# Local q and k of a sparse attention loaded in slices of every eighth token, and batch 0 masked through TensorE

## The chip, the core and the metric

The kernel runs on one core of a Trainium2 chip. The core has five engines that run side by side and wait for each other through semaphores: TensorE (PE; its weight loads are listed apart as PEld), VectorE (DVE), ScalarE (ACT), GpSimd (POOL) and SyncE (SP). DMA transfers are issued from the queues of SP, ACT and POOL and carried by 16 DMA engines. SBUF is the working memory of 128 partitions, PSUM the memory that TensorE writes its results to. The metric is the device time of one execution in microseconds; lower is better. The kernel before takes 322.0 us in the median of 8 runs (321.19 to 323.04).

## The reference

Two stages, one after the other. First a causal attention over 8 batches, 8 heads, 576 tokens and head dimension 64, in which heads 0 to 3 see only the last 32 tokens ("local") and heads 4 to 7 see every 32nd token ("strided"):

```
scores = scale * q @ k^T
rel = pos[:, None] - pos[None, :]
mask_local = (rel >= 0) & (rel < 32)
mask_strided = (rel >= 0) & (pos[None, :] % 32 == pos[:, None] % 32)
attn = softmax(where(mask, scores, -1e9));  y = attn @ v
```

Then the heads of a token are put side by side (4608 tokens by 512), and an MLP follows: h = x @ w_in (512 by 2048), g = h * tanh(softplus(h)) (the function Mish), out = g @ w_out (2048 by 512). Inputs and output are float32; the kernel computes in bfloat16.

## The kernel before

**Tiling of the attention.** Strided heads: token 8p + j lies in partition p (72 partitions, PN) and slice j (8 slices, CS), so that two slices of 64 elements make 128 columns. Their scores are 16 units of 72 by 72. Local heads: six windows of 96 queries against 128 keys (WQ, NW), for two pairs of heads, 12 units. Scores are made by `qk`, with keys on the partitions: PE multiplies kT by qT into PSUM, and ACT applies exp on the way to SBUF (P_s, P_l). `mask` multiplies P by a 0/1 mask on DVE. `pv` (one slice or window) and `pv2` (two) multiply P by v, with a column of ones that gives the denominator; DVE takes the reciprocal and scales into x_s or x_l. `xt` transposes x on PE, and ACT copies it into xT, the MLP's input.

**How q and k come to be transposed.** PE needs q and k with the head dimension on the partitions. Batch 0 and 1 are transposed on PE (`t_step`, `t_step_loc0`) with a copy from PSUM that puts the tokens in order. From batch 2 on DMA transposes do it: `transpose_str` issues two for the strided heads, of 16 units of 80 rows, and `transpose_loc` four for the local heads (k and q for two head pairs), each of six tiles of 96 consecutive tokens, straight into kTl and qTl. For that `load_qk_loc` loads local q and k of batch 0 and 1 with six consecutive tokens in a partition (96 partitions, rows of 1,536 bytes), and of later batches with token 96i + p in partition p (rows of 256 bytes). `cast_qk_loc` turns float32 into bfloat16 in the order that the transpose wants. The strided q and k come in through POOL's queue and are cast by the DMA (`load_qk_str`).

**Stages.** The order of every queue is written out by hand. A head part does the attention of batch 0. Then nine blocks t = 0 to 8 of 512 tokens follow. In block t PE first runs `mlp1(t)` (x @ w_in, eight groups, Mish on ACT), then `mlp2(t)` (g @ w_out, 16 groups), and between mlp2's groups the steps of the attention of batch t + 1 are put in (`attn_steps`). In block 0 PE also transposes batch 1, from the seventh entry of mlp1's list on. After mlp1's first group in block t >= 1, q and k of batch t + 1 are cast and `transpose_loc(t + 1)` is issued; after its third group v is cast and loaded, and `load_qk_str` is issued on POOL's queue (in block 1 for batches 3 and 4). In each such attention the first steps are the strided scores, their exp and their masks.

**POOL and SP in the early part.** Each queue runs in its own order. On POOL: memsets of P_l, loads of local q and k of batch 0 (lq0), memsets of rows 64 to 79 of ks and qs, a one-row copy `held` that waits for v of batch 0, the loads of w_in, casts of v, loads of batch 1's strided q and k, half of w_out, casts of batch 1's local q and k, and after a second `held` the other half of w_out. On SP: strided q and k of batch 0 in four loads (st0, which DVE casts into ks and qs), v, local q and k of batch 1, later all local and v loads, the DMA transposes and the output stores.

Of the kernel before, what the change touches and what calls it, by code (L numbers as in the profile page):

```python
# [18 lines left out]
CL, PL = 6, 96  # L19
# [5 lines left out]
def _consts():  # L25
# [5 lines left out]
    c = np.zeros((128, 128 + WQ + PN), np.float32)  # L31
    c[:, 0:128] = np.eye(128)
    c[:, 128:128 + WQ] = (rel >= 0) & (rel < STRIDE)
    c[:PN, 128 + WQ:] = (p[:, None] % 4 == p[None, :] % 4) & (p[:, None] <= p[None, :])
# [4 lines left out]
def kernel(ctx, tc, q, k, v, moe_w_in, moe_w_out, out):  # L39
# [15 lines left out]
    consts = const.tile([128, 128 + WQ + PN], BF16, name="consts_sb")  # L55
    ident = consts[:, 0:128]
    loc = consts[:, 128:128 + WQ]
    stm = consts[0:PN, 128 + WQ:128 + WQ + PN]
    vl32 = const.tile([128, 4, NW, D], F32, name="vl32")
    vs32 = const.tile([128, 4, CS, D], F32, name="vs32")  # L60
    ql32 = const.tile([128, 4, CL, D], F32, name="ql32")
    kl32 = const.tile([128, 4, CL, D], F32, name="kl32")
    ql = [const.tile([128, CL, 4, D], BF16, name=f"ql{i}") for i in range(2)]
    kl = [const.tile([128, CL, 4, D], BF16, name=f"kl{i}") for i in range(2)]
# [36 lines left out]
    def load_qk_loc(b):  # L101
        for dst, src in ((kl32, k), (ql32, q)):
            if b < 2:
                nc.sync.dma_start(
                    dst[0:PL].rearrange("p h j d -> p h (j d)"),
                    src[b, 0:4].rearrange("h (p j) d -> p h (j d)", j=CL),
                )
            else:
                nc.sync.dma_start(
                    dst[0:PL].rearrange("p h i d -> p (h i) d"),  # L110
                    src[b, 0:4].rearrange("h (i p) d -> p (h i) d", p=PL),
                )
# [40 lines left out]
    def cast_qk_loc(b, e_k, e_q):  # L153
        for e, dst, src in ((e_k, kl, kl32), (e_q, ql, ql32)):
            if b < 2:
                cast(e, dst[b % 2][0:PL].rearrange("p j h d -> p h j d"), src[0:PL])
            else:
                to = by_tile(dst[b % 2])
                for hp in range(2):
                    cast(  # L160
                        e, to[:, hp].rearrange("p i e d -> p e i d"), src[0:PL, 2 * hp:2 * hp + 2]
                    )

    def by_tile(x):

        return x[0:PL].rearrange("p j h d -> p (j h d)").rearrange(
            "p (t i e d) -> p t i e d", t=2, i=NW, e=2
        )

    def transpose_str(b):  # L170
        for src, dst in ((ks, kTs), (qs, qTs)):
            nc.sync.dma_start_transpose(
# [311 lines left out]
    with tc.manual_schedule():  # L484
# [43 lines left out]
        for i in range(3):  # L528
            a.qk([("s", i)], i)
# [131 lines left out]
```

The softmax here doesn't subtract the row's maximum and nothing guards it: scores larger than these inputs give would overflow.

## Time and profile before

| what | value |
|---|---|
| median of 8 runs | 322.0 us |
| the profiled execution's own time | 323.04 us |
| its span | 321.3 us |
| PE busy | 298.9 us (93%) |
| DVE busy | 127.7 us (40%) |
| ACT busy | 172.6 us (54%) |
| POOL busy | 41.3 us (13%) |
| first matmul of mlp1 | 26.9 us |
| first matmul of block 1, block 2, block 3 | 63.84, 100.03, about 132.6 us |

The span reaches from the program's first instruction to its last; the execution's own time has 1.7 us more around it. A profile's line gives the line of the code, the engine, the operation and the tiles as "out<-in". A wait is written "engine line <- what ended it: us in total, times, longest us". The chain of waits is followed back from the last instruction, at each step to what released it. In a table by stretches, each row has the stretch, its length, the busy time of each engine shown with its number of instructions, the clock that TensorE was granted (1.00 is full), the mean busy share of the DMA engines and the GB/s that they moved. In a timeline, each row has the start, the length, the engine (a name that ends in q is its queue), the operation, and in brackets the idle time before it and what ended it.

### The profile page before, as it was taken

What the parts mean: (1) busy time and instruction counts of PE and PEld (TensorE: products, weight loads), DVE (VectorE), ACT (ScalarE), POOL (GpSimd) and SP (SyncE); (2) the same over time, 40 slices, a digit from 0 to 9 for tenths busy, and PEclk for the clock granted to TensorE, in tenths of its full rate; (3) what the DMA queues carried; (4) which work ended last, traced back from release to release, by engine and by line L of the source; (5) the groups of instructions that cost most, each with busy time, mean ns of one, the idle gap of its engine ahead of it and who ended that gap; (6) DMA issues with size and microseconds to landing.
All of it is one profiled execution on the core that took longest, in us unless ns stands there. A gap on an engine that the chain in (4) does not pass through costs nothing.

```text
span 321.3 us, 5827 instructions
## 1 busy us (share of the span) xinstructions
PE 298.9 (93%) x2448; PEld 159.8 (50%) x2488; DVE 127.7 (40%) x332; ACT 172.6 (54%) x195; POOL 41.3 (13%) x50
## 2 busy tenths in 40 slices
PE   0678998999799999999999999999999999999996
PEld 0564455544345445544578655445544554444444
DVE  6672168600567038802880288028811830000000
ACT  2574563476437574656466646664667456315601
POOL 9288030145000000200020000000000000000000
PEclk9999999999889999999999999999999999999999
DMA  6999999999999999899989995896550101011012
GB/s 170 216 231 205 222 213 191 172 243 196 177 184 223 155 157 202 206 123 188 228 120 206 185 201 100 167 183 152 92 111 0 67 13 55 0 65 65 2 54 76
DMA packets 103114, 46.72 MB, mean 145 GB/s; under 512 B 85168, under 2 KB 95728, under 8 KB 103088
## 3 DMA queue, kind: packets, MB, share of 16 engines
q1 hardware_dynamic: 91648, 37.22, 64.6%
q0 software_dynamic: 11152, 8.92, 18.5%
q8 instruction: 19, 0.31, 0.4%
q10 hardware_dynamic: 288, 0.21, 0.2%
q14 instruction: 7, 0.06, 0.1%
HBM read 38.34 MB, written 9.44 MB: 149 GB/s over the span
## 4 chain that ended last, share of the span: by engine, by line
PE 81%; DVE 11%; DMA 4%; issue 2%; ACT 1%; SPq 0%; ACTq 0%
PE psh L428 38%; PE pso L467 27%; PE po L305 4%; PE pso L449 4%; DMA qTl<-ql 3%; PE ps L278 3%; DVE x_l L317 3%; DVE x_s L317 2%; PE trx L344 2%; DVE Pl L289 1%; DVE rden L316 1%; DVE ks L151 1%; DMA st<-in_k_dram 1%; PE trx L354 1%; PE tr L207 1%
## 5 line engine op out<-in xcount | busy, mean ns | idle before, releaser
L428 PE MATMUL psh<-xT,w_in 128*128 128x512 bf16 (+1 forms) x628 | 126.3, 359 | 0.8 <-issue 0.2
L467 PE MATMUL pso<-w_out,gT 128*128 128x512 bf16 x485 | 123.1, 382 | 1.7 <-issue 0.6
L433 ACT ACTIVATE gT<-psh 128x1024 bf16<-128x1024 f32 x72 | 73.6, 1023 | 44.0 <-PE psh L428 42.7
L428 PEld LDWEIGHTS <-w_in 128*128 128x128 bf16 x640 | 62.7, 98 | 62.2 <-issue 1.3
L467 PEld LDWEIGHTS <-gT 128*128 128x128 bf16 x512 | 43.9, 98 | 39.6 <-issue 1.1
L289 DVE TENSOR_TENSOR Ps<-Ps,consts_sb 72x864 bf16<-72x864 bf16 (+1 forms) x24 | 13.2, 551 | 89.7 <-ACT Ps L283 89.7
L149 ACT COPY xT<-trx 128x576 bf16<-128x576 bf16 x32 | 20.1, 639 | 37.7 <-PE trx L354 28.2
L474 ACT COPY osb<-pso 128x1024 f32<-128x1024 f32 x16 | 16.2, 1012 | 24.3 <-PE pso L467 13.8
L283 ACT ACTIVATE Ps<-ps 72x864 bf16<-72x864 f32 (+1 forms) x24 | 18.5, 803 | 15.3 <-PE ps L278 15.3
L316 DVE RECIPROCAL rden<-po 72x4 f32<-72x4 f32 (+1 forms) x100 | 17.4, 174 | 20.8 <-PE po L305 20.7
L317 DVE TENSOR_TENSOR x_s<-po,rden 72x256 bf16<-72x256 f32 x56 | 23.6, 421 | 1.9
L151 DVE COPY osb<-pso 128x512 f32<-128x512 f32 (+1 forms) x2 | 1.1, 558 | 54.5 <-PE pso L449 54.5
L283 ACT ACTIVATE Pl<-ps 128x960 bf16<-128x960 f32 (+1 forms) x24 | 18.7, 806 | 3.6 <-PE ps L278 3.5
L305 PEld LDWEIGHTS <-Ps 72*128 72x128 bf16 x256 | 14.2, 103 | 12.6 <-DVE Ps L289 2.6
L317 DVE TENSOR_TENSOR x_l<-po,rden 96x256 bf16<-96x256 f32 x44 | 18.5, 421 | 1.5
L305 PE MATMUL po<-vs,Ps 72*128 72x65 bf16 x256 | 17.9, 203 | 0.7 <-DVE x_s L331 0.5
L97 POOL DMA_DIRECT2D ks<-in_k_dram x7 | 6.2, 884 | 83.3 <-DMA kTs<-ks 83.3
L305 PE MATMUL po<-vl,Pl 128*128 128x65 bf16 x192 | 12.9, 201 | 2.2 <-DVE x_s L317 0.7
L449 PE MATMUL pso<-w_out,gT 128*128 128x512 bf16 (+1 forms) x79 | 14.0, 336 | 0.1
L305 PEld LDWEIGHTS <-Pl 128*128 128x128 bf16 x192 | 9.9, 103 | 6.5 <-DVE x_l L317 1.8
L289 DVE TENSOR_TENSOR Pl<-Pl,consts_sb 128x960 bf16<-128x960 bf16 (+1 forms) x24 | 13.1, 545 | 0.0
L449 PEld LDWEIGHTS <-gT 128*128 128x128 bf16 x80 | 7.8, 98 | 6.2
(70 smaller groups left out, 180.5 us busy)
## 6 DMA issues: line engine op xcount, KB each, us to landing
out_dram<-osb SPq DMA_DIRECT2D x16, 512.0 KB, 3.3
vl<-in_v_dram SPq DMA_DIRECT2D x7, 768.0 KB
vs<-in_v_dram SPq DMA_DIRECT2D x8, 576.0 KB
kl<-in_k_dram SPq DMA_DIRECT2D x7, 576.0 KB, 8.8
ql<-in_q_dram SPq DMA_DIRECT2D x7, 576.0 KB, 10.6
w_out<-in_moe_w_out_dram POOLq DMA_DIRECT2D x4, 512.0 KB, 15.4
ks<-in_k_dram POOLq DMA_DIRECT2D x7, 288.0 KB, 8.4
qs<-in_q_dram POOLq DMA_DIRECT2D x7, 288.0 KB, 9.8
```

What stands on the lines that cost most here:

```text
L149: nc.scalar.copy(out_, in_)
L278: nc.tensor.matmul(ps[:, e, o:o + w], lhsT=lhsT, rhs=rhs, start=True, stop=True)
L283: nc.scalar.activation(pt[0:n, :, 0:nw], ps[0:n, :, o0:o0 + nw], AF.Exp, scale=scale)
L289: meng.tensor_tensor(out=pm, in0=pm, in1=mk[0:n, :].unsqueeze(1).unsqueeze(1).to_broadcast([n, 2, nu, w]), op=ALU.mult,)
L305: nc.tensor.matmul(po[:, h, :], lhsT=pt[0:n, c0:c0 + 128], rhs=rhs, start=True, stop=True,)
L316: nc.vector.reciprocal(rden[0:m, :], po[0:m, :, D])
L317: nc.vector.tensor_tensor(out=dst.rearrange("p (h d) -> p h d", h=4), in0=po[0:m, :, 0:D], in1=rden[0:m, :].unsqueeze(2).to_broadcast([m, ...
L428: nc.tensor.matmul(ps[:, u, o:o + n], lhsT=w_in[:, cc, fc * 128:(fc + 1) * 128], rhs=xT[:, cc, a:a + n], start=(cc == 2), stop=(cc == 1),)
L433: nc.scalar.activation(gT[:, 2 * g:2 * g + 2, :], ps[:], AF.Mish)
L449: nc.tensor.matmul(p, lhsT=gT[:, fc, 128 * ot:128 * ot + 128], rhs=w_out[:, fc, c0:c1], start=(fc == 0), stop=(fc == 15),)
L467: nc.tensor.matmul(p[:, ot % 2, :], lhsT=gT[:, fc, 128 * ot:128 * ot + 128], rhs=w_out[:, fc, :], start=(fc == 0), stop=(fc == 15),)
L474: nc.scalar.copy(osb[:], p[:])
```

## The change

Local q and k take the layout of the strided ones in every batch: token 8p + j in partition p, slice j, 72 partitions with rows of 2,048 bytes. A DMA transpose then gives 16 units of 80 columns (two head pairs times eight slices) instead of tokens in order. There are two transposes a batch, into new tiles kTu and qTu, and a new step `in_order` copies them, reading every 80th column, into kTl and qTl. In block 1 this copy is on POOL, in later blocks on DVE, between mlp1 and mlp2. kl and ql have one buffer each instead of two. Batches 0 and 1, still transposed on PE, use eight slices of 72 instead of six of 96.

In the head part, the masks of batch 0 are no longer multiplied on DVE: a matmul of the identity by a bias matrix (0 or -30000, new columns of the constants) first fills the accumulator, and the scores are added to it without a new start. The copies of batch 0's local transposes go to DVE for head pair 0 and to ACT for pair 1. v's strided cast moves from DVE to POOL, the local v cast from ACT to POOL, the memsets of ks[1] and qs[1] from the start to block 0, and the order of pv, qk and xt steps is new.

```diff
     def load_qk_loc(b):
         for dst, src in ((kl32, k), (ql32, q)):
-            if b < 2:
-                nc.sync.dma_start(... 96 partitions, j=CL ...)
-            else:
-                nc.sync.dma_start(... "h (i p) d -> p (h i) d", p=PL ...)
+            nc.sync.dma_start(
+                dst[:].rearrange("p h j d -> p h (j d)"),
+                src[b, 0:4].rearrange("h (p j) d -> p h (j d)", j=CS),
+            )
...
+    def transpose_units(src, dst):
+        nc.sync.dma_start_transpose(dst[:, 0:16 * SU].rearrange("c (u n) -> c u n", u=16), src)
     def transpose_loc(b):
-        for hp in range(2):
-            for src, dst in ((kl, kTl[:, hp, 32:32 + S]), (ql, qTl[:, hp, :])):
-                nc.sync.dma_start_transpose(...)
+        for src, dst in ((kl, kTu), (ql, qTu)):
+            transpose_units(src[:].rearrange("p h j e d -> p (h j e d)"), dst)
+    def in_order(eng):
+        for src, dst in ((kTu, kTl[:, :, 32:32 + S]), (qTu, qTl[:])):
+            cast(
+                eng, dst.rearrange("c h (p j) -> c h p j", j=CS),
+                src[:].rearrange("c (h j n) -> c h n j", h=2, j=CS)[:, :, 0:PN, :],
+            )
...
+        def bias(self, kind, i, i_acc):
+            n, w, mk = (128, WQ, locb) if kind == "l" else (PN, PN, stmb)
+            nu = len(PARTS[kind][i])
+            ps = acc(i_acc, "ps")
+            for e in range(2):
+                nc.tensor.matmul(
+                    ps[:, e, 0:nu * w].rearrange("p (u c) -> p u c", u=nu), lhsT=ident[0:n, :],
+                    rhs=mk.unsqueeze(1).to_broadcast([n, nu, w]), start=True, stop=True,
+                )
+            return ps
-        def qk(self, parts, i_acc):
+        def qk(self, parts, i_acc, ps=None):
...
-                        nc.tensor.matmul(ps[:, e, o:o + w], lhsT=lhsT, rhs=rhs, start=True, stop=True)
+                        nc.tensor.matmul(
+                            ps[:, e, o:o + w], lhsT=lhsT, rhs=rhs, start=first, stop=True,
+                            skip_group_check=not first,
+                        )
...
+        sb = [a.bias("s", i, i) for i in range(3)]
         for hp in range(2):
             h = 2 * hp
             cast(Dv, qs[0][0:PN, h:h + 2, :], st0[1][:, h:h + 2, :])
             t_step(0, "s", "q", hp, Dv if hp else Sc)
         for i in range(3):
-            a.qk([("s", i)], i)
-        a.mask("s", 0, Dv)
-        cast(Dv, vs[0][0:PN, :, :, 0:D], vs32[0:PN])
-        a.mask("s", 1, Dv)
-        for x in (ks, qs):
-            Po.memset(x[1][64:SU], 0.0)
+            a.qk([("s", i)], i, sb[i])
+        cast(Po, vs[0][0:PN, :, :, 0:D], vs32[0:PN])
         Po.tensor_copy(held[:], vs[0][0:1, 3, 0, 0:4])
...
         cast_v_loc(0, Po, 0, 3)
+        cast_v_loc(0, Po, 3, 6)
...
         for hp in range(2):
-            t_step_loc0(kl0, kTl[:, hp, 32:32 + S], hp, Sc)
-        a.pv2("s", 0, 0)
-        a.mask("s", 2, Dv)
-        a.pv2("s", 2, 1)
+            t_step_loc0(kl0, kTl[:, hp, 32:32 + S], hp, Sc if hp else Dv)
+        lb = [a.bias("l", i, i) for i in range(2)]
         for hp in range(2):
-            t_step_loc0(ql0, qTl[:, hp, :], hp, Sc)
+            t_step_loc0(ql0, qTl[:, hp, :], hp, Sc if hp else Dv)
+        a.pv2("s", 0, 2)
+        a.qk([("l", 0)], 0, lb[0])
...
         def rest_of_w_out():
...
+            for x in (kl, ql):
+                Po.memset(x[64:SU], 0.0)
             cast_qk_loc(2, Po, Po)
...
+                at[1] += [lambda x=x: Po.memset(x[1][64:SU], 0.0) for x in (ks, qs)]
...
                     transpose_loc(t + 1)
+                    if t == 1:
+                        in_order(Po)
...
+            if t > 1 and t + 1 < B:
+                in_order(Dv)
             for i, g in enumerate(mlp2(t, gT, out_accs, fc_major=(t == 0), spare=spare)):
```

## The prediction

> **What bounds the kernel now.** I read the page first, then the waits of TensorE (PE), the chain of waits, the table by stretches, and the timelines of SP and POOL around the one long wait.
>
> ```profile
> span 321.3 us, 5827 instructions
> ...
> PE 298.9 (93%) x2448; PEld 159.8 (50%) x2488; DVE 127.7 (40%) x332; ACT 172.6 (54%) x195; POOL 41.3 (13%) x50
> ...
> DMA  6999999999999999899989995896550101011012
> ...
> PE 81%; DVE 11%; DMA 4%; issue 2%; ACT 1%; SPq 0%; ACTq 0%
> ```
>
> PE carries the end: 81% of the chain. DMA is full until about 240 us, yet holds only 4% of it. So time can be won or lost only where PE stands still, and the waits of PE show two such places: the start (8.5 us before the first transposes) and this one:
>
> ```profile
> PE ps L278 <- DMA qTl<-ql: 1.9, 1, 1.9
> ```
>
> ```profile
> 63.84:100.03 36.19, 33.94 (x265) 16.68 (x268) 12.28 (x38) 19.81 (x23) 8.03 (x10) 0.95 1.23 205
> 100.03:132.60 32.57, 32.08 (x265) 16.12 (x269) 15.86 (x43) 19.74 (x22) 1.41 (x2) 1.00 1.19 183
> ```
>
> Columns: stretch, length, busy PE, PEld, DVE, ACT, POOL, granted clock, DMA share, GB/s. Blocks 1 and 2 hold the same 265 matmuls, but block 1 takes 3.62 us more and has a mean clock of 0.95. The stretches inside it (length, PE, clock, DMA share, GB/s) tell why:
>
> ```profile
> 84.00:86.00 2.00, 0.74 (x17) 1.00 1.30 185
> 86.00:88.00 2.00, 2.00 (x10) 0.64 1.35 179
> 88.00:90.00 2.00, 2.00 (x10) 0.51 1.36 175
> ```
>
> PE waits from 83.3 to 85.2 us, then runs at half clock until 90.3. The wait costs 1.9, the clock about 1.7. And why is the transpose late?
>
> ```profile
> 73.91 0.72 POOL L97 DMA_DIRECT2D ks<-in_k_dram  x1
> 74.62 0.71 POOL L97 DMA_DIRECT2D qs<-in_q_dram  x1
> 75.32 0.70 POOL L97 DMA_DIRECT2D ks<-in_k_dram  x1
> 76.02 0.70 POOL L97 DMA_DIRECT2D qs<-in_q_dram  x1
> ```
>
> The fourth local transpose was issued at 74.80 and landed at 85.2; the third (73.49) landed at 78.3. Between them POOL's queue launched the strided loads of batches 3 and 4, which held about 91% of the DMA engines from 76 to 84 us.
>
> The start:
>
> ```profile
> 4.46 1.80 POOL L534 MEMSET ks<- 16x2048 bf16 x1
> 4.82 4.28 DVE L151 CAST ks<-st 72x1024 bf16<-72x1024 f32 x2 [1.13 <-DMA st<-in_k_dram]
> 6.20 2.35 POOL L534 MEMSET qs<- 16x2048 bf16 x1
> 9.02 1.27 DVE L151 CAST qs<-st 72x1024 bf16<-72x1024 f32 x2
> ```
>
> Two equal casts take 2.18 us each beside POOL's memsets and 0.68 without.
>
> **What the Trainium skill says.** "TensorE: Matmul & The Clock Gate", Part 1: after an idle window of some 3.4 us the clock halves, and as long a busy one restores it. The trace agrees on the halved clock and its length (86.7 to 90.3), though the wait was only 1.9 us. "SBUF — State Buffer", "SBUF: two separate sides": DVE in a two-port mode and GpSimd lock one port pair for a whole instruction; the 2.18 against 0.68 us agrees. "DMA: Bandwidth & Descriptors", "Why a DMA increments its semaphore by 16 and not by 1": a load runs on the largest number of engines up to 16 that divides the slowest dimension, so 72 partitions use 12 and 96 use 16. The completion records agree: each st load has 12 late increments (4.2 to 4.8 us for the first). "VectorE: DVE Perf Modes", "Mode 1× (REGULAR)": one element a cycle at 0.96 GHz whatever the stride. The strided copies kTl<-tr give 758 ns for 576 elements.
>
> **The change part by part.**
>
> *Strided loads of block 1.* in_order on POOL stands ahead of these four loads in POOL's queue, and waits for both new transposes. They can no longer collide. The transposes are issued after the two output stores (66.67 and 69.44 now, the second gated by the copy ending at 65.05). Bytes: 2 x 1,280 packets of 256 B for 4 x 576, +11%; the isolated pair of strided transposes at 222.09 landed both by 228.6 (6.5 us), the isolated local four at 231.91 by 238.6 (6.7), so the DMA time is equal. Three of four landed by 78.3 now; with the queue ahead of them shorter (below) I put both at 75 to 78. The copies have no row: 1,152 strided elements on POOL, nearest the 826 ns for 768 of vl, so 1.2 us each; GpSimd's worse case, twice that, 2.5. Done at 77.5 to 80.5, at worst 83; PE asks at 83.1. The wait goes, and with it the slow clock: **-3.6** (from 0, if the copies are late, to -3.6).
>
> *Local loads of batches 2 to 7.* 4,608 packets of 256 B (median 29 to 31 ns; kl and ql alone took 206.0 to 213.9 = 7.9 us) become 576 of 2,048 B on 12 engines: 48 an engine x 84 to 121 ns = 4.0 to 5.8 us. DMA gets 2 to 4 us a batch, SP's issues of 8 to 10 us shrink. PE waits for no load there, so 0 by itself; it pays for the rest.
>
> *in_order on DVE, blocks 2 to 6.* Two copies of 1,152 elements: 1.2 us at one a cycle plus about 0.1, 2.6 a block; casts of 72x1024 (676) for 96x768 (548) add 0.5. The cover:
>
> ```profile
> 117.30 0.60 DVE L289 TENSOR_TENSOR Ps<-Ps,consts_sb 72x864 bf16<-72x864 bf16 x1 [13.68 <-ACT Ps L283]
> ```
>
> DVE is idle 13.7 us before the first mask of each block. Behind the waiting copy stands only that mask, and behind it PE's first pv. The transposes landed at 115.9, 146.4, 176.3 and 206.0; masks at 117.3, 149.8, 182.4 and about 215. One copy (1.3) after the last landing just fits at 117.3, without the DMA relief. With two batches' relief (4 to 8 us by then), less up to 2 us of DMA idle while POOL holds back its loads, block 2 fits even 3.6 us earlier: **0** (bound: the second rival).
>
> *Start.* The four st loads landed at 4.8, 6.1, 7.5 and 8.9. Without memsets the k casts end at 6.8 instead of 9.1, the q casts at 9.6 instead of 10.3. But six bias matmuls (2,304 columns; PE is at half clock here, 427 ns for 512 columns at 27 us) add 1.9 us from 7.4 to 9.3, so qk starts near 11.1 as now. Then local k, landed at 13.5, holds PE in both kernels. From there: masks gone from DVE (0.60 + 0.60 + 0.44 + 0.64 + 0.64 + 0.34 = 3.3) and vs' cast moved to POOL (1.2), but PE gets another 1.9 us of bias. PE's work from 13.5, at half clock: transposes 2.4, bias 1.9, qk 1.5, pv 4.3, x transposes 2.5, plus waits: mlp1 starts at about 25.7 to 26.2, not 26.9. It is not kept: w_out's first part landed at 41.45 and PE asks at 42.86, slack 1.4. POOL now issues w_in after its own cast of vs (landed 13.3, cast 1.9), 0.5 us later, and engines 0 to 11 carry a third more bytes each of lq, kl and ql. I put that landing at 42.0 to 43.0, so **-0.3** (-1.2 to +1.0).
>
> *Block 0.* Memsets of kl and ql (1.8 each) follow POOL's loads at 44.5, beside DVE's cast of vs (44.92, 1.22). If locked out, the mask at 46.53 is up to 0.9 late and PE has 0.6 of slack: **+0.3** (0 to +0.9). The transposes, 8 x 72 for 6 x 96, take 0.42 either way (rows L207, L220). Casts on POOL end near 62, before they are asked for.
>
> *POOL's copies beside the first masks of block 1*: **+0.2** (0 to 0.9).
>
> Sum: -3.6 - 0.3 + 0.3 + 0.2 = **-3.4**. It is made against the profiled execution (span 321.3, 1.7 us around it: 323.04, the top of the runs shown). Carried to the median 322.0 it gives **318.6**.
>
> **Rivals.** (1) *The start pays.* If w_out isn't as late as I fear, or the denser PE gains full clock before mlp1 (its first four matmuls cost 0.43 instead of 0.21), another 1 to 2 us: 316.5 to 317.5. For: 3.3 us of masks are gone. Against: DMA is full from 6 us. (2) *Slower: DVE stands before a transpose.* With PE 3.6 us earlier, block 2's mask is due at 113.7, and qTu must land by 112.4. If the relief is under 2 us a batch, landing stays near 115: a wait of about 2.6 and the half clock after it, 1.7, in block 2, and since PE is early again, part of it in block 3 and 4: 3.6 gained, 5 to 6 lost, 323.5 to 324.5. It decides when the landing is later than the mask's due time less 1.3. For: DMA share is above 1.2 in those blocks. Against: 31 ns packets. (3) *Even*: the copies on POOL take above 2.5 us, or block 2 takes back what block 1 gave: 321 to 322.5.
>
> **Numbers.** A difference under 0.3% (1.0 us) can't be told from none. Forecast 0.53 (317.5 to 320), rival 1 0.14, even 0.15, slower 0.18. Faster 0.68 (the forecast, rival 1 and 0.01 of even), same 0.14, slower 0.18. The range leaves out most of rival 2 and the far end of rival 1: 316.6 to 322.8.
>
> **What would show it.** Right: no PE wait for a local transpose near 83 us, clock 1.00 in 84 to 90, block 1 at about 32.6 us; POOL's four loads after 77; two DVE copies of some 1.3 us each ending before the mask. Wrong: DVE's first mask waiting behind in_order with PE idle and a clock near 0.5 in block 2 or 3; POOL copies above 3 us; a wait of pso on w_out near 42 us; mlp1 starting after 27.

## The result, and the profile after

The changed kernel takes 327.8 us in the median of 11 runs (326.15 to 332.21), against 322.3 us before on the same chips: a ratio of 1.017 (95% interval 1.014 to 1.020). It is slower by 1.7%, on the other side of the forecast of 318.6 us, and outside its range. Ratios here leave out executions that lie over 1.5% above the fastest of the same kernel; medians don't.

The page of the changed kernel (span, busy shares, DMA in 40 slices, the chain):

```profile
span 326.1 us, 5884 instructions
...
PE 303.1 (93%) x2483; PEld 161.5 (50%) x2524; DVE 140.6 (43%) x340; ACT 170.5 (52%) x191; POOL 54.2 (17%) x58
...
DMA  6999999999999999999989975995480101011011
...
PE 72%; DMA 16%; DVE 7%; issue 1%; SPq 1%; POOL 1%; ACT 0%; POOLq 0%; ACTq 0%
```

PE does nearly the same work, but its part of the chain falls from 81% to 72%, and DMA's rises from 4% to 16%: PE now stands more, for data. Where, the table by blocks tells. Before, the row of block 0, which the prediction did not show:

```profile
26.90:63.84 36.94, 35.48 (x318) 18.86 (x323) 18.21 (x46) 17.96 (x21) 8.65 (x10) 1.00 1.24 201
```

After, blocks 0, 1 and 2:

```profile
27.77:72.07 44.30, 38.24 (x325) 19.82 (x331) 20.50 (x47) 17.66 (x21) 22.59 (x19) 0.96 1.16 202
72.07:104.56 32.49, 32.00 (x265) 16.08 (x269) 12.20 (x37) 19.80 (x23) 11.44 (x11) 1.00 1.10 205
104.56:137.04 32.48, 31.99 (x264) 16.07 (x268) 18.86 (x45) 19.75 (x22) 1.87 (x2) 1.00 1.05 174
```

Block 1 went from 36.19 to 32.49 us, as forecast: -3.7. But mlp1 starts 0.87 later, and block 0 takes 7.36 us more. Block 2 is the same: before, it ran from 100.03 to 132.51 us, so it took 32.48 and not 32.57. 0.87 + 7.36 - 3.70, plus 0.3 in all that follows, is the 4.8 us between the spans. The waits of PE, after:

```profile
PE po L315 <- DVE x_s L327: 4.1, 2, 3.0
PE tr L228 <- DMA lq<-in_k_dram: 2.7, 1, 2.7
PE ps L285 <- ACT Ps L293: 1.3, 1, 1.3
```

The first is the large one. DVE's timeline tells what held x_s up, before and after:

```profile
52.70 0.94 DVE L151 CAST vl<-vl 128x768 bf16<-128x768 f32 x1
```

```profile
59.86 0.96 DVE L151 CAST vl<-vl 128x768 bf16<-128x768 f32 x1 [3.48 <-DMA vl<-in_v_dram]
```

The local v of batch 1 landed at 59.8 us instead of 52.6. DVE's cast stood for it, the reciprocals behind that cast stood too, and PE behind them; the clock was then granted at 0.73 and 0.50 from 62 to 66 us:

```profile
62.00:64.00 2.00, 0.89 (x8) 0.50 (x7) 1.93 (x6) 0.00 (x0) 0.85 (x1) 0.73 1.73 191
64.00:66.00 2.00, 1.78 (x12) 0.97 (x12) 1.16 (x5) 0.00 (x0) 1.53 (x2) 0.50 0.93 184
```

These waits and that clock make some 4.6 us of block 0. The third wait, 1.3 us, is a table load. ACT's timeline before and after:

```profile
43.58 1.28 ACT L283 ACT_TABLE_LOAD   x1
```

```profile
47.92 1.28 ACT L293 ACT_TABLE_LOAD   x1 [2.10 <-PE ps L285]
```

Before, the table of Exp was loaded as soon as ACT had finished its last Mish: the load waits for a semaphore of DVE, long since given. After, it waits for PE's scores of batch 1, and PE waits for it. The other 1.4 us of block 0 is a longer half clock at the start of mlp1 (10 matmuls 427 ns apart instead of 4), which a second execution of the kernel before, below, has as well.

### The profile page after: what moved, and what is told of

It is laid out like the page before. It is cut to its first block, busy times and chain, and to the rows that moved or that the text cites. A ratio compares the mean times of both kernels' runs of the same rounds, so it can differ in the third digit from the quotient of the medians.

```text
span 326.1 us, 5884 instructions
## 1 busy us (share of the span) xinstructions
PE 303.1 (93%) x2483; PEld 161.5 (50%) x2524; DVE 140.6 (43%) x340; ACT 170.5 (52%) x191; POOL 54.2 (17%) x58
## 2 busy tenths in 40 slices
DMA packets 79826, 47.16 MB, mean 145 GB/s; under 512 B 58808, under 2 KB 68408, under 8 KB 79800
## 3 DMA queue, kind: packets, MB, share of 16 engines
q1 hardware_dynamic: 68360, 37.62, 57.3%
## 4 chain that ended last, share of the span: by engine, by line
PE 72%; DMA 16%; DVE 7%; issue 1%; SPq 1%; POOL 1%; ACT 0%; POOLq 0%; ACTq 0%
PE psh L438 34%; PE pso L477 26%; DMA vl<-in_v_dram 12%; PE pso L459 4%; DMA w_in<-in_moe_w_in_dram 4%; PE po L315 4%; PE ps L285 3%; DVE x_l L327 2%; DVE x_s L327 2%; DVE rden L326 1%; PE trx L354 1%; DVE Pl L299 1%; PE trx L364 1%; DVE vl L151 1%; POOL vl L151 0%
## 5 line engine op out<-in xcount | busy, mean ns | idle before, releaser
L438 PE MATMUL psh<-xT,w_in 128*128 128x512 bf16 (+1 forms) x628 | 127.7, 362 | 0.8 <-issue 0.2
L477 PEld LDWEIGHTS <-gT 128*128 128x128 bf16 x512 | 43.9, 98 | 39.6 <-issue 1.1
L149 ACT COPY xT<-trx 128x576 bf16<-128x576 bf16 x31 | 19.6, 638 | 41.5 <-PE trx L364 33.8
L299 DVE TENSOR_TENSOR Ps<-Ps,consts_sb 72x864 bf16<-72x864 bf16 (+1 forms) x21 | 11.6, 551 | 43.1 <-ACT Ps L293 43.1
L484 ACT COPY osb<-pso 128x1024 f32<-128x1024 f32 x16 | 16.2, 1012 | 22.7 <-PE pso L477 13.9
L327 DVE TENSOR_TENSOR x_s<-po,rden 72x256 bf16<-72x256 f32 x60 | 25.2, 421 | 2.1
L293 ACT ACTIVATE Ps<-ps 72x864 bf16<-72x864 f32 (+1 forms) x24 | 18.5, 803 | 12.7 <-PE ps L285 12.6
L151 DVE COPY osb<-pso 128x512 f32<-128x512 f32 (+1 forms) x2 | 1.1, 558 | 54.5 <-PE pso L459 54.5
L151 DVE COPY kTl<-kTu 128x1152 bf16<-128x1152 bf16 x5 | 6.4, 1277 | 29.1 <-DMA kTu<-kl 29.1
L327 DVE TENSOR_TENSOR x_l<-po,rden 96x256 bf16<-96x256 f32 x42 | 17.7, 421 | 1.4
L103 POOL DMA_DIRECT2D ks<-in_k_dram x7 | 5.5, 790 | 73.8 <-DMA kTs<-ks 73.8
L151 DVE CAST vl<-vl 128x768 bf16<-128x768 f32 x12 | 10.9, 942 | 3.5 <-DMA vl<-in_v_dram 3.5
```

Source lines behind the costliest of these rows:

```text
L149: nc.scalar.copy(out_, in_)
L151: eng.tensor_copy(out_, in_)
L293: nc.scalar.activation(pt[0:n, :, 0:nw], ps[0:n, :, o0:o0 + nw], AF.Exp, scale=scale)
L299: meng.tensor_tensor(out=pm, in0=pm, in1=mk[0:n, :].unsqueeze(1).unsqueeze(1).to_broadcast([n, 2, nu, w]), op=ALU.mult,)
L327: nc.vector.tensor_tensor(out=dst.rearrange("p (h d) -> p h d", h=4), in0=po[0:m, :, 0:D], in1=rden[0:m, :].unsqueeze(2).to_broadcast([m, ...
L438: nc.tensor.matmul(ps[:, u, o:o + n], lhsT=w_in[:, cc, fc * 128:(fc + 1) * 128], rhs=xT[:, cc, a:a + n], start=(cc == 2), stop=(cc == 1),)
```

## The experiments

Fifteen further kernels were run, and both kernels of the comparison a second time. Times are medians, ratios are against runs of the kernel before on the same chip, with 95% intervals; most kernels have four executions, the kernels with more are named. Figures of blocks and waits are those of one profiled execution of each. In all nineteen profiles blocks 3 to 7 take the same times within 0.05 us, e_late and e_fix apart: what differs lies in the start and in blocks 0 to 2.

### The change in halves

`e_b2only`: the kernel before with the new layout from batch 2 on alone.

```diff
 def load_qk_loc(b):
...
-            else:
-                nc.sync.dma_start(
-                    dst[0:PL].rearrange("p h i d -> p (h i) d"),
-                    src[b, 0:4].rearrange("h (i p) d -> p (h i) d", p=PL),
-                )
+            n, c = (PL, CL) if b < 2 else (PN, CS)
+            nc.sync.dma_start(
+                dst[0:n, 0:256 * c].rearrange("p (h x) -> p h x", h=4),
+                src[b, 0:4].rearrange("h (p j) d -> p h (j d)", j=c),
+            )
...
+                    if t == 1:
+                        in_order(Po)
...
+            if t > 1 and t + 1 < B:
+                in_order(Dv)
```

> The kernel before with the new local layout from batch 2 on alone (loads of 2,048-byte rows, two transposes, in_order); batches 0 and 1 and the start as before. The start theory (what is late comes from batches 0 and 1 or from the new order of the start): block 0 stays near 37 us, vl of batch 1 lands at 52 to 54 us, block 1 takes 32.6 us, time 318 to 319. The packet theory (kl and ql of batch 2, in rows of 2,048 bytes, crowd out the 256-byte packets of vl of batch 1): vl lands at 57 us or later, block 0 takes over 40 us, time 321 to 324.

Measured: 323.7 us in 20 executions, ratio 1.005 (1.002 to 1.008). vl of batch 1 landed at 48.7, so the packet theory falls; but block 0 took 39.08 us, not about 37, and the 318 to 319 us of the start theory aren't met either. Block 1 took 34.13 and block 2 33.01: half of the gain in block 1 is there against the first execution of the kernel before, none against the second (below), a wait of 1.6 us stays at its first masks, and the time is already slightly worse.

`e_layout` is the changed kernel with the old head part:

```diff
-        sb = [a.bias("s", i, i) for i in range(3)]
...
         for i in range(3):
-            a.qk([("s", i)], i, sb[i])
-        cast(Po, vs[0][0:PN, :, :, 0:D], vs32[0:PN])
+            a.qk([("s", i)], i)
+        a.mask("s", 0, Dv)
+        cast(Dv, vs[0][0:PN, :, :, 0:D], vs32[0:PN])
+        a.mask("s", 1, Dv)
...
```

`e_head` is the kernel before with the new head part, the same lines the other way round. `e_after_l96` is the changed kernel with the old layout in batches 0 and 1:

```diff
+            n, c = (PL, CL) if b < 2 else (PN, CS)
             nc.sync.dma_start(
-                dst[:].rearrange("p h j d -> p h (j d)"),
-                src[b, 0:4].rearrange("h (p j) d -> p h (j d)", j=CS),
+                dst[0:n, 0:256 * c].rearrange("p (h x) -> p h x", h=4),
+                src[b, 0:4].rearrange("h (p j) d -> p h (j d)", j=c),
             )
...
-            Po.dma_start(dst, src[0, 0:4].rearrange("h (p j) d -> p h (j d)", j=CS))
+            Po.dma_start(dst, src[0, 0:4].rearrange("h (p j) d -> p h (j d)", j=CL))
...
```

> The changed kernel with the old start: masks of batch 0 on DVE, v's strided cast on DVE, the second half of the local v cast on ACT, memsets at the start, steps in the old order. The layout is the new one in every batch. Theory of the 12 engines (72-partition loads of batches 0 and 1 fill twelve of sixteen engines ahead of w_in): the last part of w_in lands at 35 us or later, vl of batch 1 at 57 to 60, time 323 to 327. Theory of the start's order (POOL holds w_in back for v's cast): w_in lands near 34, vl near 53, time 318 to 319.5.

> The kernel before with the new start alone (bias matmuls, casts on POOL, copies on two engines, new order); the local layout stays the old one everywhere, so the wait of block 1 (1.9 us and the half clock after it) stays. Theory of the start's order: w_in lands at 36 or later, vl of batch 1 at 56 or later, block 0 over 40 us, time 325 to 330. Theory of the 12 engines: w_in lands at 34 to 35, vl at 52 to 55, time 321.5 to 324, what is over 322 from the table of Exp, which now is loaded behind the scores of batch 1 (up to 1.4 us).

> The changed kernel with batches 0 and 1 alone in the old local layout (96 partitions, six slices), all else as changed. Theory of the 12 engines: w_in lands at 34 to 35, vl of batch 1 at 52 to 55, time 318 to 321. Theory of the start's order: w_in at 36 to 37, vl at 57 to 60, time 325 to 328.

Measured: 327.3 (1.019, 1.010 to 1.028), 325.3 (1.010, 1.004 to 1.017) and 325.9 (1.011, 1.003 to 1.019). Neither theory fits: each half alone is slower, and where the early part was mended (block 0 at 38.73 and 39.37 us, vl at 48.7 and 46.8), the time was lost in block 2 instead. e_head has no loss in block 2; it keeps the collision (block 1 at 36.29) and has the wait for the table in block 0. The waits of PE in e_layout and in e_after_l96:

```profile
PE po L292 <- DVE Ps L276: 2.6, 1, 2.6
```

```profile
PE po L329 <- DVE Ps L313: 3.0, 2, 2.8
```

That is the rival that the prediction gave 0.18: DVE's first mask standing behind in_order, which waits for the transposes.

### What made block 1 slow

`e_hold` is the kernel before and, in block 1, one copy of four elements ahead of the strided loads:

```diff
                     if t + 2 < B:
                         load_v(t + 2)
+                    if t == 1:
+                        Po.tensor_copy(held[:], qTl[0:1, 1, 0:4])
                     for b in range(max(3, t + 2 + (t > 1)), min(t + 4, B)):
                         load_qk_str(b)
```

`e_loads_first` is the changed kernel with in_order of block 1 behind those loads:

```diff
                     transpose_loc(t + 1)
-                    if t == 1:
-                        in_order(Po)
...
                     for b in range(max(3, t + 2 + (t > 1)), min(t + 4, B)):
                         load_qk_str(b)
+                    if t == 1:
+                        in_order(Po)
```

> The kernel before with one line more: at block 1 POOL copies four elements of qTl, and so stands until the last local transpose has landed, before it launches the strided loads of batches 3 and 4. Old layout and old start throughout. Collision theory (these loads alone made the transpose late): the PE wait near 83 us and the half clock go, block 1 takes 32.5 to 32.8 us. If the early part is bound by the sum of DMA work, what is won comes back as a wait for a local transpose in block 2 and the time is 320.5 to 322; if not, it is 318 to 319. Layout theory (it is the two larger transposes that removed the wait): block 1 stays above 35 us.

> The changed kernel with POOL's in_order of block 1 behind the strided loads of batches 3 and 4 in its queue instead of ahead of them. Collision theory: qTu lands at 84 us or later, POOL's copies end after 88, PE waits 3 us or more near 90 us, time 329 to 333. Relief theory (fewer packets are what removed the wait, and holding the loads only wastes DMA time): qTu lands before 82, no wait, time 325 to 327.5.

Measured: e_hold 320.4 us in 20 executions, ratio 0.995 (0.992 to 0.997), the best kernel of this study; e_loads_first 327.1, ratio 1.012 (1.003 to 1.020). Block 1 of e_hold, and block 1 of e_loads_first:

```profile
65.45:97.94 32.49, 32.38 (x270) 16.08 (x268) 12.19 (x38) 19.80 (x23) 8.26 (x11) 1.00 1.22 205
```

```profile
67.75:104.05 36.30, 34.21 (x269) 16.70 (x268) 12.28 (x37) 19.80 (x23) 12.17 (x11) 0.95 1.07 196
```

With the old layout and the loads held back, block 1 takes 32.49; with the new layout and the loads ahead, 36.30, with a PE wait of 2.0 us and the half clock after it. The collision is shown from both sides, and the layout has no part in it. e_hold missed the 318 to 319 us expected where nothing comes back in block 2: block 2 has no wait, but its block 0 took 38.97 us. e_loads_first missed 329: PE's wait at the copies was 2.0 us and not 3 or more, and its block 2 has no wait, since PE was late already.

### A second execution of both kernels, and the table of Exp

> The kernel before itself, to see how much of its block 0 and block 1 is one execution's chance. The first profile had block 0 at 36.94 us and block 1 at 36.19. If half clock at the start of mlp1 falls by chance, block 0 is between 36.5 and 39.5 and block 1 takes back a part (33.5 to 36.3), with the sum between 71 and 74.

Measured: 322.4 us. Blocks 0 and 1:

```profile
26.90:65.28 38.38, 36.92 (x318) 19.22 (x323) 18.40 (x46) 17.96 (x21) 9.15 (x10) 1.00 1.25 196
65.28:99.41 34.13, 32.28 (x265) 16.14 (x268) 12.19 (x38) 19.80 (x23) 8.03 (x10) 1.00 1.22 199
```

Block 0 is 1.44 us longer and block 1 2.06 shorter than in the execution that the prediction read: the wait for qTl is 1.5 us, and no slow clock follows it. So the 3.6 us to be won in block 1 were the upper end; 1.6 (34.13 less 32.49) to 3.7 is what the two executions hold. The prediction read them in the slowest of its eight executions (323.04) and took them from the median. e_hold, whose median is 1.35 below that of the kernel before, fits the lower end.

> The changed kernel itself, unchanged, to see a second execution in full. If the late vl of batch 1 (59.8 us) is a property of the kernel, it lands at 57 to 61 us again and PE waits 4 us near 60. If it is one execution's chance, it lands at 47 to 53, and the time is lost in another place: a wait of 2.5 to 3 us in block 2 as the two relatives of it showed, with block 0 at 39 to 41 us.

Measured: 326.9 us, and another picture. vl landed at 51.9, block 0 took 40.17, block 1 32.49, block 2 34.08. DVE and PE at the first masks of block 2:

```profile
117.60 1.27 DVE L151 COPY kTl<-kTu 128x1152 bf16<-128x1152 bf16 x1 [11.24 <-DMA kTu<-kl]
119.00 1.27 DVE L151 COPY qTl<-qTu 128x1152 bf16<-128x1152 bf16 x1
120.20 1.11 DVE L299 TENSOR_TENSOR Ps<-Ps,consts_sb 72x864 bf16<-72x864 bf16 x2
```

```profile
PE po L315 <- DVE Ps L299: 1.5, 1, 1.5
```

So the changed kernel loses its time in one of two places: at vl in block 0, or, where PE comes through block 0 in time, at the transposes of batch 3 in block 2.

`e_preload` is the changed kernel with an explicit load of the table behind the last mlp1 group of block 0:

```diff
+            if t == 0:
+                Sc.preload_act_table(AF.Exp)
             for i, g in enumerate(mlp2(t, gT, out_accs, fc_major=(t == 0), spare=spare)):
```

> The changed kernel with an explicit load of the Exp table after the last mlp1 step of block 0, as it happened before the change on its own. If each stall of block 0 counts: the wait of 1.35 us behind the first scores of batch 1 goes and the time falls to 326.0 to 326.7. If vl of batch 1, which lands after it, decides: the wait for x_s grows by the same 1.3 us and the time stays at 327.5 to 328.

Measured: 328.0 us (1.017, 1.009 to 1.025): nothing won. The wait of 1.3 us for the table is gone from the list, and in its profile, the slowest of its four executions (330.6), this one has come up in block 2:

```profile
PE po L315 <- DVE Ps L299: 4.9, 2, 4.6
```

### Mending one part at a time

`e_late` is the changed kernel with in_order behind the first two masks:

```diff
                     at = attn_steps(t + 1, x, y)
+                    if t > 1:
+                        at[1].append(lambda: in_order(Dv))
...
-            if t > 1 and t + 1 < B:
-                in_order(Dv)
```

`e_split` is the changed kernel with every local load of q and k split (lq in the same way):

```diff
-            nc.sync.dma_start(
-                dst[:].rearrange("p h j d -> p h (j d)"),
-                src[b, 0:4].rearrange("h (p j) d -> p h (j d)", j=CS),
-            )
+            for p in (slice(0, 64), slice(64, PN)):
+                nc.sync.dma_start(
+                    dst[p].rearrange("p h j d -> p h (j d)"),
+                    src[b, 0:4].rearrange("h (p j) d -> p h (j d)", j=CS)[p],
+                )
```

`e_fix` is e_after_l96 with the edits of e_preload and e_late.

> The changed kernel with in_order of blocks 2 to 6 behind the first two masks of each block on DVE instead of ahead of them. Gate theory (the two copies tie the first masks to the landing of the transposes, and PE then stands in block 2): the wait of the first pv near 120 us goes or falls below 0.7 us, and the time falls by 1 to 3 us to 325 to 327; in an execution in which block 0 is late by itself nothing is won. If the transposes themselves are what PE lacks, the wait reappears one step on, at the scores of the local part, with the same length, and the time stays at 327 to 328.

> The changed kernel with each load of local q or k (72 partitions) issued as two, one of 64 partitions and one of 8, and nothing else. Theory of the 12 engines: the 64 partitions spread over sixteen engines, local k of batch 0 lands at 13.5 to 14.5 us instead of 15.4, the last part of w_in at 33.5 to 35 instead of 36.8 to 38.2 with its sixteen completions less than 2.5 us apart, mlp1 starts at 26.2 to 27.2, and the time falls by 1 to 3 us to 325 to 327. If the number of bytes is what counts, all of these stay within 0.5 us.

> The changed kernel with three parts mended at once: batches 0 and 1 in the old layout of 96 partitions, the Exp table loaded after the last mlp1 step of block 0, in_order of blocks 2 to 6 behind the first two masks. If these three are all that lost time, block 0 takes 37 to 39 us, block 1 and block 2 take 32.5 to 33, and the time is 318 to 321, below the kernel before. If the loss is the sum of DMA work ahead of block 2, a wait stays in block 1 or 2 and the time is 322 to 326.

Measured: 337.9 (1.051, 1.046 to 1.055), 332.9 (1.033, 1.027 to 1.038) and 336.3 us (1.045, 1.038 to 1.051). All three were expected to gain. e_late, PE's waits and DVE in block 2:

```profile
PE ps L285 <- DVE qTl L151: 8.1, 5, 1.6
```

```profile
121.96 0.60 DVE L299 TENSOR_TENSOR Ps<-Ps,consts_sb 72x864 bf16<-72x864 bf16 x1 [0.17 <-ACT Ps L293]
122.49 1.26 DVE L151 COPY kTl<-kTu 128x1152 bf16<-128x1152 bf16 x1
123.67 1.26 DVE L151 COPY qTl<-qTu 128x1152 bf16<-128x1152 bf16 x1
```

Behind the masks the two copies (2.5 us) stand in front of the local scores, in each of five blocks, for 1.6 us each. That prices the cover that the prediction named: ahead of the masks the copies are free when the transposes have landed, and right behind them they are not. e_fix pays the same, and 3.1 us in block 2. e_split: local k landed by 15.6, no earlier than in the changed kernel (15.4); PE waited 1.7 instead of 2.7 us for it because it came later itself. The last part of w_in came at 38.7 instead of 36.8, and PE waited 6.8 us in block 0. Splitting the loads, which also doubles their number in the queues, doesn't mend the start.

### Which transfer is late

`e_gate` is the changed kernel with kl and ql of batch 2 held on SP:

```diff
             Po.memset(x[0][64:SU], 0.0)
-        load_qk_loc(2)
...
             load_w_out(2, 4)
             load_qk_str(2)
+            nc.sync.dma_start(gate[:], w_out[0:1, 8, 0:256])
+            load_qk_loc(2)
```

`e_l96_gate` is e_after_l96 with this edit and that of e_preload; `e_head_hold` is e_head with the edits of e_hold and e_preload.

> The changed kernel with the loads of kl and ql of batch 2 held on SP until the third part of w_out has landed (a four-row copy that waits for it stands ahead of them), nothing else. Order theory (SP's loads of batch 2 run ahead of ks, qs of batch 2 and vl of batch 1): vl of batch 1 lands at 45 to 50 us, qs of batch 2 at 58 to 61 instead of 63 to 66, the DMA share of 60 to 72 us rises above 1.05, the transposes of batch 3 land by 117.5, and the time is 321 to 325. Start theory (half a megabyte less by 27 us is carried along): the transposes of batch 3 land at 118.5 or later and the time stays at 326 to 328.5.

> The changed kernel with batches 0 and 1 in the old layout of 96 partitions, the Exp table loaded after the last mlp1 step of block 0, and the same hold of kl and ql of batch 2; in_order stays ahead of the masks. Order theory: no PE wait above 0.7 us in blocks 0 to 2, block 3 starts at 130 to 132, time 319 to 321.5. If the transposes of batch 3 are late for another reason (SP's own queue order, the copies behind their landing), a wait of 1.5 to 4 us stays in block 2 and the time is 322.5 to 326.

> The kernel before with the new start, with the Exp table loaded after the last mlp1 step of block 0 and with POOL's hold of the strided loads in block 1; old layout everywhere, so no in_order. If the new start is worth its 0.3 us of PE once its two side effects are gone, and block 2 can take it: 319 to 320.5. If early DMA decides, PE comes earlier and waits in block 2 for a local transpose: 320.5 to 323.

Measured: 327.3 (1.016, 1.008 to 1.024), 326.2 (1.012, 1.005 to 1.019) and 321.1 us (0.995, 0.993 to 0.998). In e_gate the transposes of batch 3 landed earlier (116.7), as the order theory said, but vl of batch 1 landed at 58.7 with kl and ql of batch 2 held back until 53.7: they are not what delays vl. The time did not move. In e_head_hold vl was late as well (block 0 at 42.30 us), with the old layout. Its 20 executions spread: 12 lie between 319.2 and 321.8, 8 between 323.6 and 327.4, and the profiled one (323.6) is of the second group. Its median is 0.3 us below that of the kernel before, with block 1 at 32.48; its mean is 0.4 above (322.4 against 322.0). e_l96_gate has the fastest start (mlp1 at 25.61), 37.63 us in block 0, 32.90 in block 1, and the earliest transposes of all kernels with the new layout. It is slow all the same. DVE and PE in block 2:

```profile
108.40 1.28 DVE L155 COPY kTl<-kTu 128x1152 bf16<-128x1152 bf16 x1 [6.00 <-DMA kTu<-kl]
115.91 1.27 DVE L155 COPY qTl<-qTu 128x1152 bf16<-128x1152 bf16 x1 [6.24 <-DMA qTu<-ql]
117.10 1.12 DVE L313 TENSOR_TENSOR Ps<-Ps,consts_sb 72x864 bf16<-72x864 bf16 x2
```

```profile
117.75 0.62 PE L329 MATMUL po<-vs,Ps 72*128 72x65 bf16 x8 [3.58 <-DVE Ps L313]
```

PE was early, waited 3.58 us, and lost 2.7 more to the half clock: block 2 took 38.78 us.

### Cutting the tie

In e_after_l96, e_layout, e_preload, after_again and e_l96_gate the first pv of block 2 starts 1.84 or 1.85 us after DVE begins the copy of qTl (1.27 of copy, then the mask): a fixed distance from a landing. Leaving the copies of block 2 out cuts that tie; the local attention of batch 3 then works on batch 2's q and k.

```diff
-            if t > 1 and t + 1 < B:
+            if t > 2 and t + 1 < B:
                 in_order(Dv)
```

> The kernel of e_l96_gate without in_order in block 2: the order copies of batch 3 are left out, so its local attention is computed with batch 2's local q and k; the transposes still run. Tie theory (the first masks of block 2 stand behind copies that wait for the transposes): the wait of 3.6 us and the half clock after it go, block 2 takes 32.5 us, block 3 starts near 129 us, and the time falls by 5 to 7 us to 319 to 321. If PE lacks something else there, a wait above 1.5 us stays in block 2 and the time is 323 or more.

> The changed kernel without in_order in block 2 (the same part left out). Tie theory: no wait in block 2 in any execution; where vl of batch 1 is late in block 0 nothing changes (326 to 328), where it is not, block 3 starts at 131 to 134 and the time is 321 to 325; the median lies between, at 323 to 326. If the tie isn't what costs, the median stays at 327 to 328.5.

Measured: e_no_copy3 (on e_l96_gate) 322.3 us in 18 executions, ratio 1.001 (0.998 to 1.003), and block 2 without a wait, though its transposes landed at 115.8 again:

```profile
97.92:130.41 32.49, 32.00 (x265) 16.07 (x268) 16.40 (x43) 19.75 (x22) 1.41 (x2) 1.00 1.10 206
```

e_after_no_copy3 (on the changed kernel) 326.6 us, above the 323 to 326 expected; ratio 1.008 (1.004 to 1.011), in which the lower of two groups has most of the weight. Of its 19 executions 8 lie between 322.4 and 324.6, 11 between 326.5 and 329.7. The profiled one, of the second group, has the wait for vl in block 0 (2.2 and 1.1 us). None of the 11 runs of the changed kernel was below 326.15.

Four medians separate the two losses: the changed kernel 327.8, with the tie cut alone 326.6, with the early part mended alone (e_l96_gate) 326.2, with both 322.3. One repair by itself wins 1.2 or 1.6 us, both win 5.5: each loss hides the other, which is why one repair at a time won next to nothing. That the tie costs 3.9 us once the early part is in time is shown (e_no_copy3 against e_l96_gate). Even with both repaired the kernel is no faster than before: what was to be won in block 1 isn't seen in the median, and six of the 18 executions of e_no_copy3 lie between 325.8 and 327.5, whose cause no profile shows. That the whole second group of e_after_no_copy3 is held by vl is read from its one profile, and not shown for the rest.

## Why the prediction was wrong, point by point

Two terms failed. The start and block 0, priced at -0.3 and +0.3, cost +0.9 and +7.4 us in the profiled execution: the path from the first loads over w_in to vl of batch 1 was not in the sum. And in_order on DVE, priced at 0 because a relief of the DMA engines would bring the transposes in earlier, ties PE to a landing that did not move. Each alone is enough to lose the gain of block 1.

**Strided loads of block 1, -3.6: right in cause, upper end in size.** The wait and the half clock went. POOL, after:

```profile
79.75 2.41 POOL L151 COPY kTl<-kTu 128x1152 bf16<-128x1152 bf16 x1 [3.50 <-DMA kTu<-kl]
82.09 2.41 POOL L151 COPY qTl<-qTu 128x1152 bf16<-128x1152 bf16 x1
84.44 0.72 POOL L103 DMA_DIRECT2D ks<-in_k_dram  x1
```

The copies took 2.41 us each, at the worst end of the 1.2 to 2.5 of the prediction. The Trainium skill ("GPSIMD Engine Reference", "7. Performance pitfalls for Q7 kernels") points to that end: it says that reads of SBUF with a step above 8 bytes cost a kernel there about half as much again. The trace shows more: 2.41 us is 2.1 ns an element, twice the 1.1 of the cast of vl (826 ns for 768) that the prediction started from.

**Local loads of batches 2 to 7, "DMA gets 2 to 4 us a batch": right as packet time, wrong in its use.** The queue's line before and after:

```profile
q1 hardware_dynamic: 91648, 37.22, 64.6%
```

```profile
q1 hardware_dynamic: 68360, 37.62, 57.3%
```

64.6% of 321.3 less 57.3% of 326.1 is 20.7 us, 3.5 for each of six batches, if all of it is theirs. It did not shorten the way of the transposes. Those of batch 3 were issued from 103.5 to 108.4 us before and landed by 115.9; after, issued at 106.3 and 109.6, landed by 119.9. SP's queue before, and in e_l96_gate, whose block 2 begins 3.9 us earlier:

```profile
103.50 1.31 SPq L180 DMA_TRANSPOSE kTl<-kl  x1
108.37 1.42 SPq L180 DMA_TRANSPOSE qTl<-ql  x1
```

```profile
103.59 1.93 SPq L173 DMA_TRANSPOSE kTu<-kl  x1
105.63 2.60 SPq L173 DMA_TRANSPOSE qTu<-ql  x1
```

103.6 to 115.8 is 12.2 us, before 103.5 to 115.9 was 12.4; over all profiles it is 11.2 to 13.8 us with the old layout and 11.0 to 13.5 with the new. The transposes stand in SP's queue behind the strided ones and the output stores, and from issue to landing they take as long as before. A part of the time that was freed became idle: the DMA share (one before the last figure) from 60 to 72 us, in the kernel before and in the second execution of the changed kernel:

```profile
60.00:72.00 12.00, 11.87 (x81) 5.97 (x81) 1.71 (x6) 9.22 (x10) 4.59 (x5) 1.00 1.19 214
60.00:72.00 12.00, 11.04 (x100) 5.91 (x99) 6.51 (x21) 6.61 (x9) 8.12 (x6) 1.00 0.74 155
```

In the first execution of the changed kernel, whose loads were late there, it was 1.18.

**in_order on DVE, "0": the first of the two failed steps.** The copies take 1.28 us each, as forecast. But "block 2 fits even 3.6 us earlier" rested on the relief. Without it, the first pv of block 2 can't start before the landing of qTu plus 1.85 us, and PE asks 18.0 us into the block (116.3 in e_after_l96, which began block 2 at 98.31). It fits only where DVE can begin the copy of qTl within 16.2 us of the block's start. It began 17.7 us after it in after_again (a wait of 1.5), 19.0 in e_after_l96 (2.8) and 19.8 in e_l96_gate (3.6), but 15.4 in the first profile of the changed kernel, whose block 2 began late. The old layout has no such tie, so e_hold could keep its gain with transposes landing at 117.2, 19.3 us into block 2. This is rival 2, with its mechanism and its place as described ("if the relief is under 2 us a batch"); it deserved more of the chance, since a relief of packet time was never shown to be a relief of landing. Its size was short: in e_l96_gate the wait and the clock cost 3.6 and 2.7 us, not 2.6 and 1.7.

**Start, -0.3: wrong in sign, by one term.** mlp1 began at 27.77 (27.21 to 28.66 in six other executions of the same start) instead of 26.6. The PE work was priced well: the prediction's parts add up to 12.6 us from the landing of local k (26.1 us, so its 25.7 left no room for waits), and in the new head part mlp1 begins 11.7 to 12.8 us after it. What failed is "local k, landed at 13.5, holds PE in both kernels": it landed at 15.4 (14.6 to 15.9 in seven executions; with batches 0 and 1 in the old layout under the same head part 13.7 to 14.5 in six, where mlp1 begins between 25.61 and 26.92), and vs at 15.1, behind which POOL's queue now launches w_in (at 17.2 instead of 15.4). The first two stretches of the two kernels:

```profile
0.00:15.00 15.00, 5.10 (x90) 4.14 (x91) 10.22 (x20) 5.97 (x9) 8.06 (x12) 1.00 0.91 191
15.00:27.00 12.00, 8.86 (x133) 7.19 (x135) 8.32 (x21) 8.02 (x12) 10.73 (x14) 1.00 1.21 224
```

```profile
0.00:15.00 15.00, 5.64 (x70) 3.88 (x70) 5.62 (x17) 5.39 (x7) 3.94 (x9) 1.00 0.88 175
15.00:27.00 12.00, 11.05 (x174) 8.15 (x175) 7.92 (x20) 5.88 (x8) 10.66 (x15) 1.00 1.07 204
```

15 x 191 + 12 x 224 is 5.55 MB by 27 us, after it 5.07, in e_after_l96 5.63. Half a megabyte is 2.4 us of a DMA that moves 205 GB/s, and w_in's last part came 3.0 us later (33.8 to 36.8), with w_out and vl of batch 1 behind it. The prediction had put w_out's first part at 42.0 to 43.0; it landed at 44.9. Of the sixteen completions of that last part, four came at 31.4 to 31.6 us and twelve at 34.7 to 36.8 (before, fifteen at 31.4 to 32.6 and one at 33.8), which agrees with the page "DMA: Bandwidth & Descriptors" of the Trainium skill, named in the prediction; but e_split, which spread the same bytes, moved still less (15 x 173 + 12 x 180 is 4.76 MB), so why the 72-partition loads cost bytes stays open.

**Block 0, +0.3: +7.4 in this execution, the second failed step.** The term itself was right: DVE's cast of vs took 2.62 us beside POOL's memset of kl (46.93 to 48.73) instead of 1.22, and cost nothing, since the exp it leads to was late. Two things were not in the sum. The first is vl of batch 1 (above), which hangs on w_in through the gate on SP; its own path was never priced. That gate explains 3.0 of its 7.2 us: vl was issued at 38.2 instead of 35.2. The other 4.2 lie in the transfer itself, and mostly in the last of its sixteen completions: fifteen were there by 54.5 us and the last at 59.8 (47.6 and 52.6 before, 50.6 and 51.9 in the second execution of the changed kernel). The second is the table load. Taking the masks of batch 0 off DVE took away the wait for DVE that the load had carried; it now carries the wait for the scores, and can't run ahead of them. The waits that the program gives to ACT's instructions show that ahead of any run, and the prediction did not read them. Both are real waits, but in e_preload, whose PE came through block 0 in 39.12 us, more than was won there was paid in block 2.

**POOL's copies beside the first masks of block 1, +0.2:** nothing in the changed kernel, where PE came late (block 1 at 32.49). In e_b2only PE came earlier, and DVE's two masks stood beside POOL's copy of qTl (82.62 to 85.03):

```profile
83.23 2.78 DVE L290 TENSOR_TENSOR Ps<-Ps,consts_sb 72x864 bf16<-72x864 bf16 x2 [18.45 <-ACT Ps L284]
```

Two masks take 1.2 us otherwise. That fits the lock of the port pair that the prediction cited for the casts: the two masks end 1.0 us after POOL's copy. PE waited 1.6 us, beyond the 0.9 of the prediction.

What stays open: why vl lands late in some executions. It made PE wait 2 us or more in six of the fourteen profiles with the new head part (the changed kernel, e_late, e_split, e_gate, e_head_hold, e_after_no_copy3), and in none of the five with the old one, which is few to tell by. In three of the six a single completion came 5.3 to 8.5 us behind the other fifteen. It happened with kl and ql of batch 2 held back (e_gate) and with the old layout (e_head_hold), so neither is needed for it. And one reading of the prediction was loose, without weight here: the page shows the DMA engines near full until about 193 us, not 240.

## What to carry to other kernels

A shorter transfer is worth what its landing moves, and the landing may be set by the issue queue. Before booking DMA relief, ask which instruction is queued in front of the issue, and whether that one moves. Price a new copy between a transfer and its user by the distance it forces: landing, plus copy, plus what is queued behind the copy, against the moment PE asks, and at the earlier start that the rest of the change is meant to bring. Where two waits can each hide the other, a repair of one shows nothing; look at several executions before naming the one that counts. The cheap gain here, half a per cent, was one line that keeps bulk loads out of the way of the transfer that is needed next.

## What the runs showed of the hardware

- A table load on ACT takes 1.28 us, and the wait it carries decides whether that is hidden. Dropping an instruction of another engine (a mask on DVE) moved the wait from an old event to the scores, and PE stood 1.35 us.
- The half clock after a wait doesn't follow from the wait's length: 2.79 us of wait in block 2 of e_after_l96 left the clock at 1.00, while 2.65 in e_layout brought it to 0.50 from 121 to 123 us, and 1.9 in the kernel before to 0.51. At the start of mlp1 between 4 and 12 matmuls were 427 ns apart in executions of like kernels. "TensorE: Matmul & The Clock Gate" of the Trainium skill, Part 1, says that the window of activity is free-running, so that the number of slow matmuls differs from run to run; the traces agree.
- A strided copy of 1,152 elements per partition took 1.28 us on DVE and 2.41 us on POOL.
- 23% fewer DMA packets in all (103,114 to 79,826), and larger ones, left the bytes moved by 84 us no higher (16.7 MB after, 17.1 before).
